# Gated decode attention: scores on TensorE from K with d on the partitions, and a softmax of partial maxima

## The chip, the cores and the metric

One Trainium2 chip, one of its cores. The metric is the device time of the whole kernel in microseconds, the median of several runs of one program. All arithmetic on the large tensors is float32.

## What is computed

One token goes through two attention blocks, and a gate mixes their outputs. Block A has 16 heads, each with its own K and V cache of 8192 keys; block B has 16 query heads that share 8 K and V caches, two heads to a cache. The head size is 256, the model width 448.

```python
x = A_x                                            # 1 x 1 x 448
g = sigmoid((x * gate_w).sum(-1, keepdims=True))
q = (x @ wq).reshape(16, 256)                      # in each block
p = softmax(q @ k.T * 256 ** -0.5)                 # over 8192 keys, each head
o = p @ v                                          # 256 numbers, each head
block = o.reshape(4096) @ wo
return g * A + (1 - g) * B
```

Each K and V cache of a head is 8 MB, and there are 24 of each, so 403 MB of caches and 29 MB of weights are read once and hardly any of it is used twice (only block B's, for two heads).

## The kernel before

The work is cut into 8 rounds `s`. A round has three units `u = (s, r)`: two heads of block A (`r` 0 and 1) and one cache of block B (`r` 2), with two query heads (`heads(u)` is 2 there). A unit's cache comes in four tiles `t` of 2048 keys, 2 MB each: 128 partitions with 16 keys (`ROWS`) of 256 numbers, 16 KB in one run on each partition. A round also needs a tile of `wq` (1792 KB; the first round's comes as two halves) and one of `wo` (1792 KB).

All these loads are issued by SyncE, in one list that lines 225 to 251 write out: K tiles run in `K_ORDER`, V tiles follow `LAG` = 7 tiles later in `V_ORDER`, and the next round's `wq` stands after the ninth K tile. Every tile gets the next of 11 slots of one ring (`slot`, line 72), so load n + 11 can be issued only when load n has been used. The loop at line 254 goes through the same list and writes down the work of the other engines in that order.

- `project` (line 130, TensorE): x, spread over 128 columns (`xb`, line 96), is the stationary operand and 256 columns of `wq` move, so that q appears alike on all partitions of PSUM.
- `score` (line 146, VectorE): for each of a tile's 16 keys per partition one `tensor_tensor_reduce` of 256 elements, K times q, summed into one column of `S`; two of them in block B. The profile shows each as two instructions, the operation and a read of its accumulator.
- `maximum` (line 157, VectorE), and `softmax` (line 163): GpSimd takes the maximum over the partitions (line 166) and makes it a bias, ScalarE computes Exp with a sum (line 172), GpSimd adds the sums over the partitions (line 174). One maximum stands for all 8192 keys of a head, so V can be used only when the unit's four K tiles have been scored.
- `weights` (line 178): the reciprocal of the sum times the gate, on partitions 0, 32, 64 and 96 (`pick`).
- `attend` (line 188, TensorE): for each of a tile's 16 keys per partition a column of `pr` is the stationary operand (1 or 2 columns) and 256 numbers of V move; the output goes to one of four partition groups (0, 32, 64, 96) of `o` in turn.
- `take` (line 199) copies `o` to SBUF, `finish` (line 203) adds the four groups with the weights and lays the result on the partitions, `emit` (line 213) multiplies by `wo` into `Y`, again in four groups of 112 columns.

At the end come the last V tile in three pieces of 8, 4 and 4 keys (`LAST_CUT`), two of four parts of the last `wo`, then `finish` and `emit` of the last unit, four copies of `Y` to one partition and the store (lines 309 to 319). A float32 matmul appears in the profile as two MATMUL and two LDWEIGHTS instructions.

## Time and profile before

| | |
|---|---|
| median of 3 runs | 1052.37 us (1052.14 to 1052.56) |
| the profiled execution, its own time | 1052.65 us |
| its span, first to last instruction | 1050.6 us |
| HBM read | 432.02 MB, 411 GB/s over the span |
| mean granted TensorE clock | 0.656 |
| engines' instructions | 13046 |

The page gives an engine's busy time, share of the span and count of instructions; for a DMA queue, its packets, megabytes and share of the time of 16 DMA engines. Queue q1 is SyncE's; the two queues called "instruction" bring the engines' own instructions. A stretch of time is one row: its bounds, its length, the busy time of PE (matmul), PEld (weight load), DVE (VectorE), ACT (ScalarE) and POOL (GpSimd) with their counts, the granted clock of TensorE, the mean share of the DMA engines that was busy, and GB/s. In a timeline a row is start, length, engine, line, operation, output and inputs, and in brackets the idle time before it and what ended it; equal instructions that follow each other are merged, with their count. SPq is the sequencer that issues SyncE's DMAs; for the DMA of a chain, the length is the time from issue to landing.

### The profile page before, as it was taken

How to read it: one execution, taken by the hardware profiler on the slowest of the kernel's cores; microseconds unless marked ns; L12 is line 12 of the kernel's file. 1: busy time of each engine (PE TensorE's matmuls, PEld its weight loads, DVE VectorE, ACT ScalarE, POOL GpSimd, SP SyncE). 2: the span in 40 equal slices, each digit the busy share in tenths (PEclk: the TensorE clock that was granted, in tenths of full speed). 3: DMA queues.
4: the chain of work that ended last, by engine and by line, in shares of the span. 5: the costliest groups of instructions: out<-in, count | busy, mean ns of one | idle time of the engine just before them, and what ended most of it. 6: DMA issues, size and time to landing. Idle time of an engine off the chain costs nothing.

```text
span 1050.6 us, 13046 instructions
## 1 busy us (share of the span) xinstructions
PE 430.7 (41%) x3969; PEld 184.2 (18%) x3969; DVE 721.3 (69%) x4187; ACT 26.1 (2%) x116; POOL 25.1 (2%) x77
## 2 busy tenths in 40 slices
PE   4053232733328333273433634336343353343355
PEld 3031010411105111041110411103111131011012
DVE  5998765686747867568675695855958559576760
ACT  0000000000000000000000000000000000000000
POOL 0000000000000000000000000000000000000000
PEclk8576566755556555576555876558666696666778
DMA  9999999999999999999999999999999999999971
GB/s 376 426 426 426 424 427 428 425 426 425 427 427 427 428 423 427 427 427 428 425 424 428 427 426 426 422 429 428 428 423 428 427 428 426 423 420 428 428 297 42
DMA packets 31031, 432.85 MB, mean 412 GB/s; under 512 B 3697, under 2 KB 3698, under 8 KB 4594
## 3 DMA queue, kind: packets, MB, share of 16 engines
q1 hardware_dynamic: 30818, 432.03, 97.5%
q8 instruction: 31, 0.51, 0.2%
q14 instruction: 38, 0.31, 0.1%
q10 hardware_dynamic: 144, 0.00, 0.0%
HBM read 432.02 MB, written 0.00 MB: 411 GB/s over the span
## 4 chain that ended last, share of the span: by engine, by line
DMA 88%; DVE 11%; PE 1%; issue 0%; ACT 0%; SPq 0%; ACTq 0%
DMA slot<-in_b_k_dram 42%; DMA slot<-in_a_v_dram 19%; DMA slot<-in_b_v_dram 15%; DMA slot<-in_a_k_dram 12%; DVE junk L153 10%; DMA slot<-in_wq_dram 0%; PE q L136 0%; DVE S L153 0%; PE o L196 0%; PE Y L218 0%; PE q L138 0%; PE sm L112 0%; PE sm L208 0%; DVE part L125 0%; DVE pick L126 0%
## 5 line engine op out<-in xcount | busy, mean ns | idle before, releaser
L153 DVE CUSTOM_DVE_ANT_0 junk<-slot,q 128x256 f32<-128x256 f32 x2048 | 705.6, 417 | 279.7 <-DMA slot<-in_a_k_dram 155.5
L196 PE MATMUL o<-slot,pr 128*1 128x256 f32 (+1 forms) x3072 | 318.6, 586 | 593.0 <-DMA slot<-in_a_v_dram 375.3
L196 PEld LDWEIGHTS o<-slot,pr 128*1 128x1 f32 (+1 forms) x3072 | 92.7, 111 | 785.8 <-issue 317.9
L153 DVE DVE_READ_ACCUMULATOR2_ANT S<- 128x1 f32 x2048 | 169.5, 83 | 0.0
L136 PE MATMUL q<-slot,xb 128*128 128x256 f32 x192 | 58.2, 448 | 23.5 <-DMA slot<-in_wq_dram 23.5
L136 PEld LDWEIGHTS q<-slot,xb 128*128 128x128 f32 x192 | 42.9, 228 | 36.4 <-DMA slot<-in_wq_dram 22.6
L201 ACT ACTIVATE osb<-o 128x256 f32<-128x256 f32 x24 | 9.2, 383 | 746.8 <-PE o L196 746.8
L138 PE MATMUL q<-slot,xb 128*128 128x256 f32 x64 | 21.3, 418 | 0.0
L208 PEld LDWEIGHTS sm<-sel,osb 128*128 128x128 f32 x96 | 17.7, 257 | 19.1 <-issue 17.1
L208 PE MATMUL sm<-sel,osb 128*128 128x1 f32 (+1 forms) x96 | 19.7, 309 | 0.6 <-ACT osb L201 0.6
L174 POOL PARTITION_ALL_REDUCE rs<-rs x24 | 9.7, 404 | 407.3 <-ACT pr L172 313.0
L218 PE MATMUL Y<-slot,ocs 128*1 128x112 f32 x512 | 17.6, 300 | 0.3 <-ACT ocs L210 0.3
L166 POOL PARTITION_ALL_REDUCE mx<-mx x24 | 9.0, 373 | 355.9 <-DVE mx L160 346.5
L182 DVE RECIPROCAL rc<-rs 128x1 f32<-128x1 f32 (+1 forms) x24 | 3.8, 159 | 19.2 <-POOL rs L174 19.2
L138 PEld LDWEIGHTS q<-slot,xb 128*128 128x128 f32 x64 | 13.9, 217 | 2.4
L218 PEld LDWEIGHTS Y<-slot,ocs 128*1 128x1 f32 x512 | 13.6, 95 | 2.2 <-issue 0.5
L168 POOL TENSOR_SCALAR nm<-mx 128x1 f32<-128x1 f32 (+1 forms) x24 | 6.2, 257 | 235.8 <-issue 235.8
L172 ACT ACTIVATE pr<-S,nm 128x64 f32<-128x64 f32 x32 | 10.9, 342 | 37.0 <-POOL nm L168 37.0
L318 DVE COPY ys<-Y 1x112 f32<-1x112 f32 x2 | 0.5, 266 | 14.2 <-PE Y L218 14.2
L210 ACT ACTIVATE ocs<-sm 128x2 f32<-128x2 f32 (+1 forms) x24 | 4.1, 172 | 225.8 <-PE sm L208 225.8
L103 PE MATMUL o<-zero 128*128 128x256 bf16 x24 | 8.1, 338 | 0.0
L115 DVE TENSOR_SCALAR ge<-ge 128x1 f32<-128x1 f32 x1 | 0.2, 154 | 9.6 <-ACT ge L114 9.6
(25 smaller groups left out, 27.3 us busy)
## 6 DMA issues: line engine op xcount, KB each, us to landing
slot<-in_a_k_dram SPq DMA_DIRECT2D x64, 2048.0 KB, 40.1
slot<-in_a_v_dram SPq DMA_DIRECT2D x64, 2048.0 KB, 40.0
slot<-in_b_k_dram SPq DMA_DIRECT2D x32, 2048.0 KB, 39.6
slot<-in_b_v_dram SPq DMA_DIRECT2D x31, 2048.0 KB, 40.1
slot<-in_wq_dram SPq DMA_DIRECT2D x7, 1792.0 KB, 38.9
slot<-in_wo_dram SPq DMA_DIRECT2D x7, 1792.0 KB, 39.5
slot<-in_wq_dram SPq DMA_DIRECT2D x2, 896.0 KB, 10.6
slot<-in_b_v_dram SPq DMA_DIRECT2D x1, 1024.0 KB, 34.0
```

Of the source, the lines that this page charges most:

```text
L103: nc.tensor.matmul(t[:, :n], zero[:, :P], zero[:, :n], start=True, stop=False, skip_group_check=True)
L136: nc.tensor.matmul(qe, xb[:, c], w[:, c * n + e * DH:c * n + (e + 1) * DH], start=(c == 0), stop=False)
L138: nc.tensor.matmul(qe, xb[:, KF + e], w[:, KF * n:KF * n + DH], start=False, stop=True)
L153: nc.vector.tensor_tensor_reduce(jk, kt[:, j, :], Q[u][:, m * DH:(m + 1) * DH], 1.0, 0.0, OP.mult, OP.add, S[u][:, m, c0 + j:c0 + j + 1])
L166: nc.gpsimd.partition_all_reduce(mx[:, 1, :M], mx[:, 0, :M], P, bass.bass_isa.ReduceOp.max)
L168: nc.gpsimd.tensor_scalar(nm[:, :M], mx[:, 1, :M], -scale, None, op0=OP.mult)
L172: nc.scalar.activation(pr[:, :, m], S[u][:, m, :], AF.Exp, bias=nm[:, m:m + 1], scale=scale, accum_out=rs[:, 0, m:m + 1])
L174: nc.gpsimd.partition_all_reduce(rs[:, 1, :M], rs[:, 0, :M], P, bass.bass_isa.ReduceOp.add)
L196: nc.tensor.matmul(O[u][32 * g:32 * g + M, :], PR[u][:, col, :M], vt[:, j, :], start=False, stop=(col >= NCOL - NG), skip_group_check=True)
L201: nc.scalar.activation(OB[u], O[u], AF.Copy)
L208: nc.tensor.matmul(oc[:, e, :M], o[:, e::2], SEL[u][:, :M], start=True, stop=True)
L218: nc.tensor.matmul(Y[32 * g:32 * g + 1, :], OC[u][:, e, m:m + 1], wt[:, h, e, g * YN:(g + 1) * YN], start=False, stop=(last and m == heads ...
```

## The change

- **K's layout.** The host lays K out anew (`turned`): a tile is still 2048 keys and 16 KB in one run on each of 128 partitions, but a partition now holds one of 128 positions of d, for both halves `e` of d and for four groups `g` of 512 keys. V stays as it was.
- **q.** `project` has the weights as the stationary operand (128 x 128) and a column of x as the moving one, so that q comes with d on the partitions. VectorE multiplies it by -1/16 and puts it into the middle of a tile of zeros (`QB`).
- **Scores.** For each tile 8 matmuls: 32 columns of `QB` are stationary and 512 keys of K move; the four groups go to four partition groups of one PSUM tile. The columns are cut out so that the head's q falls on row `t * M + m` of the group: each tile of the unit and each head has a row of its own.
- **Softmax.** Each row gets its own maximum (here a minimum, since the scores have the other sign): VectorE reduces the 512 columns, and ScalarE computes Exp with that bias and the row's sum. GpSimd's two reductions go. `turn` transposes the exponentials by four matmuls with a selecting matrix (`SELT`), which leaves zeros in the rows of other tiles; VectorE copies the result to `pr`.
- **Attend.** The stationary operand has 4 columns (8 in block B), one for each tile and head, so that every tile and group adds into a row of its own of `o`.
- **Putting together.** After a unit's last tile, `gather`, `combine` and `column` bring the 16 minima and sums of a head together, weigh them and lay the weights on the partitions, one step later each; `reduce_o` is what `finish` was, with VectorE's copy in place of ScalarE's.
- **Order.** K and V tiles alternate: K tile i, then V tile i - 1, with the units in the order 2, 0, 1. TensorE's order in step i is scores of tile i, attend of tile i - 1, turn of tile i, then projections and what is due. The last unit is one of block A, and one part of the last `wo` follows the last V piece instead of two.
- **Small.** x is loaded from ScalarE's queue; at the end one copy takes all of `Y`, and the store reads four partitions.

```diff
-LAG = 7
-K_ORDER = [(0, 0), (0, 1), (0, 2), (0, 3), (2, 0), (1, 0), (1, 1), (2, 1), (1, 2), (1, 3), (2, 2), (2, 3)]
-V_ORDER = [(0, 0), (0, 1), (0, 2), (0, 3), (1, 0), (1, 1), (1, 2), (1, 3), (2, 0), (2, 1), (2, 2), (2, 3)]
+UNITS = [2, 0, 1]
...
+    for M in (2, 1):
+        R = M * NT
+        SELT[M] = const.tile([P, NT, NG, R], F32, name=f"selt{M}")
+        nc.vector.memset(SELT[M], 0.0)
+        for t in range(NT):
+            nc.vector.tensor_copy(SELT[M][:, t, :, t * M:(t + 1) * M], one_of[:, :, t * M:(t + 1) * M])
+        MASK[M] = const.tile([P, NT], F32, name=f"mask{M}")
+        nc.vector.tensor_reduce(MASK[M], row_of[:, :R].rearrange("p (t m) -> p t m", m=M), axis=AX.X, op=OP.add)
...
+        for m in range(M):
+            h = m if r == 2 else r
+            for e in range(2):
+                for c in range(KF):
+                    at = c * n + h * DH + e * P
+                    nc.tensor.matmul(q[:, e, m:m + 1], w[:, at:at + P], xs[:, c:c + 1], start=(c == 0), stop=False)
+                at = KF * n + e * P
+                nc.tensor.matmul(q[:, e, m:m + 1], w[:, at:at + P], xs[:, KF + h:KF + h + 1], start=False, stop=True)
+        qb = QB[s % 2, r]
+        nc.vector.tensor_scalar(qb[:, :, 16:16 + M], q[:, :, :M], -scale, None, op0=OP.mult)
...
+        sc = ps_sc.tile([P, NC4 * P], F32, name="sc")
+        qb = QB[u[0] % 2, u[1]]
         for e in range(2):
...
+            for g in range(NG):
+                nc.tensor.matmul(sc[32 * g:32 * (g + 1), :], qb[:, e, 16 - t * M:48 - t * M], kt[:, e, g, :],
+                                 start=(e == 0), stop=(e == 1), skip_group_check=True)
+        st = ST[u]
+        nc.vector.tensor_reduce(st[:, 0, t:t + 1], sc, axis=AX.X, op=OP.min)
+        px = small.tile([P, NC4 * P], F32, name="px")
+        nc.scalar.activation(px, sc, AF.Exp, bias=st[:, 0, t:t + 1], scale=-1.0, accum_out=st[:, 1, t:t + 1])
+        PX[u, t] = px
...
+        for c in range(NC4):
+            nc.tensor.matmul(pt[:, c, :, :R], px[:, c * P:(c + 1) * P], SELT[M][:, t], start=True, stop=True)
+        pr = small.tile([P, NC4, NG, 2 * NT], F32, name="pr")
+        nc.vector.tensor_copy(pr[:, :, :, :R], pt[:, :, :, :R])
+        PR[u, t] = pr
...
+        pr = PR[u, t]
+        for j in range(j0, j0 + n):
+            c, g = divmod(j, NG)
+            nc.tensor.matmul(O[u][32 * g:32 * g + R, :], pr[:, c, g, :R], vt[:, j - j0, :],
+                             start=False, stop=(t == NT - 1 and c == NC4 - 1), skip_group_check=True)
...
+    def gather(u):
+        M = heads(u)
+        gs = small.tile([P, 2, NT], F32, name="gt")
+        nc.vector.tensor_tensor(gs, ST[u], MASK[M][:, None, :].to_broadcast([P, 2, NT]), op=OP.mult)
+        GS[u] = small.tile([P, 2], F32, name="gs")
+        nc.vector.tensor_reduce(GS[u], gs, axis=AX.X, op=OP.add)
+
+    def combine(u):
+
+        M = heads(u)
+        gi = 1 if u[1] == 2 else 0
+        T = ps_s.tile([1, 2, P], F32, name="sm")
+        for k in range(2):
+            nc.tensor.matmul(T[:, k, :], GS[u][:, k:k + 1], ident, start=True, stop=True)
...
+        for m in range(M):
+            nc.vector.tensor_reduce(mn[:, m:m + 1], of_head(T[:, 0, :], m), axis=AX.XY, op=OP.min)
+        for m in range(M):
+            nc.scalar.activation(ew[:, m], of_head(T[:, 0, :], m), AF.Exp, bias=mn[:, m:m + 1], scale=-1.0)
+        for m in range(M):
+            nc.vector.tensor_tensor(es[:, m], ew[:, m], of_head(T[:, 1, :], m), op=OP.mult)
+        nc.vector.tensor_reduce(z[:, :M], es[:, :M], axis=AX.XY, op=OP.add)
+        rz = small.tile([1, 2], F32, name="rz")
+        nc.vector.reciprocal(rz[:, :M], z[:, :M])
+        nc.vector.tensor_scalar(rz[:, :M], rz[:, :M], gate[:, gi:gi + 1], None, op0=OP.mult)
+        for m in range(M):
+            nc.vector.tensor_scalar(of_head(WR[M][:, m, :], m), ew[:, m], rz[:, m:m + 1], None, op0=OP.mult)
...
+        for m in range(M):
+            nc.tensor.matmul(cl[:, m:m + 1], WR[M][:, m, :], one, start=True, stop=True)
+        SEL[u] = small.tile([P, 2], F32, name="sel")
+        nc.vector.tensor_copy(SEL[u][:, :M], cl[:, :M])
...
+    for i in range(N + 1):
+
+        if i == 0:
+            load_wq(0, 1)
+        if i < N:
+            load_k(i)
+        if i == 2:
+            load_wq(0, 0)
+        if i % PER == 5 and i // PER + 1 < NS:
+            load_wq2(i // PER + 1)
+        if 0 < i < N:
+            load_v(i - 1)
+        if i % PER == 2 and i > PER:
+            load_wo(i // PER - 1, [(0, 4)])
+        if i == N:
+            load_wo(NS - 1, [(2, 4), (0, 1)])
+            VT[N - 1] = []
+            j0 = 0
             for n in LAST_CUT:
...
+                vt = slot([n, DH], "v")
+                nc.sync.dma_start(vt, v_src(N - 1)[:, j0:j0 + n, :])
+                VT[N - 1].append((j0, n, vt))
+                j0 += n
+            load_wo(NS - 1, [(1, 2)])
...
+        if i == 0:
+            project((0, 2), W[0, 1])
+            prepare()
+        if i < N:
+            scores(*work[i], KT.pop(i))
+        if i == N:
+            u = work[N - 1][0]
+            combine(u)
+            column(u)
+            emit((u[0], 2), WO[u[0]])
+            emit((u[0], 0), WO[u[0]])
+        if i > 0:
+            u, t = work[i - 1]
+            for j0, n, vt in VT.pop(i - 1):
+                attend(u, t, j0, n, vt)
+            PR.pop((u, t))
+            if t == NT - 1:
+                take(u)
+        if i < N:
+            u, t = work[i]
+            turn(u, t)
+            if t == NT - 1:
+                gather(u)
+                if i < N - 1:
+                    at(i + 1, combine, u)
+                    at(i + 2, column, u)
+                    at(i + 3, reduce_o, u)
...
+        s = i // PER + 1
+        if s < NS:
+            for k, r in enumerate(UNITS):
+                if i % PER == 6 + k:
+                    project((s, r), W[s, 1 if r == 2 else 0])
...
+        for f, args in later.pop(i, []):
+            f(*args)
+        if i % PER == 4 and i > PER:
+            for k, r in enumerate(UNITS):
+                emit((i // PER - 1, r), WO[i // PER - 1])
...
+    reduce_o((s, 1))
+    emit((s, 1), WO[s], last=True)
+
+    ys = const.tile([P, YN], F32, name="ys")
+    nc.vector.tensor_copy(ys, Y)
+    nc.sync.dma_start(out.rearrange("a b (g n) -> (a b g) n", g=NG), ys[::32, :])
```

More of the change, by code (lines that the diff above doesn't have):

```diff
@@ L94 @@
     nc.vector.memset(xs[KR:, KF:KF + 1], 0.0)
-    xb = const.tile([P, KF + 2, P], F32, name="xb")
-    nc.vector.tensor_copy(xb, xs[:, :, None].to_broadcast([P, KF + 2, P]))
-    junk = [const.tile([P, DH], F32, name=f"junk{i}") for i in range(3)]
-    gate = const.tile([P, 2], F32, name="gate")
-    pick = const.tile([P, 2], F32, name="pick")
+    gate = const.tile([1, 2], F32, name="gate")
     def clear(t, n):
@@ L117, in prepare @@
         nc.vector.tensor_scalar(gate[:, 1:2], gate[:, 0:1], -1.0, 1.0, op0=OP.mult, op1=OP.add)
-        nc.vector.memset(pick, 0.0)
-        row = const.tile([P, 2], F32, name="row")
-        nc.gpsimd.iota(row, pattern=[[-1, 2]], base=0, channel_multiplier=1,
-                       allow_small_or_imprecise_dtypes=True)
-        part = const.tile([P, 2], F32, name="part")
-        for c in range(NG):
-            nc.vector.tensor_scalar(part, row, float(32 * c), None, op0=OP.is_equal)
-            nc.vector.tensor_add(pick, pick, part)
@@ L178, in weights, with project @@
-    def weights(u):
+    KT, VT, SC, ST, PX, PR, O, GS, SEL, OB, OC = ({} for _ in range(11))
+    def project(u, w):
+        s, r = u
+        M = heads(u)
+        q = ps_s.tile([P, 2, 2], F32, name="sm")
+        n = 2 * DH
+        for m in range(M):
[8 more added lines that the diff above has]
+        nc.vector.tensor_scalar(qb[:, :, 16:16 + M], q[:, :, :M], -scale, None, op0=OP.mult)
@@ new lines, in turn, with attend @@
+    def turn(u, t):
+        M = heads(u)
+        R = M * NT
+        pt = ps_t.tile([P, NC4, NG, 2 * NT], F32, name="pt")
+        px = PX.pop((u, t))
+        for c in range(NC4):
[3 more added lines that the diff above has]
+        PR[u, t] = pr
+    def attend(u, t, j0, n, vt):
+        R = heads(u) * NT
+        if t == 0 and j0 == 0:
+            O[u] = ps_o.tile([P, DH], F32, name="o")
+            clear(O[u], DH)
+        pr = PR[u, t]
[3 more added lines that the diff above has]
+                             start=False, stop=(t == NT - 1 and c == NC4 - 1), skip_group_check=True)
@@ L179, in weights, with take @@
+    def take(u):
+        OB[u] = small.tile([P, DH], F32, name="osb", bufs=3)
+        nc.scalar.activation(OB[u], O[u], AF.Copy)
+    def gather(u):
+        M = heads(u)
+        gs = small.tile([P, 2, NT], F32, name="gt")
[3 more added lines that the diff above has]
+    def combine(u):
         M = heads(u)
         gi = 1 if u[1] == 2 else 0
-        rc = small.tile([P, 2], F32, name="rc")
@@ L204, in finish, with reduce_o @@
+    def reduce_o(u):
         M = heads(u)
@@ L309 @@
-    finish((NS - 1, 2))
-    emit((NS - 1, 2), W[NS - 1], last=True)
-    ys = const.tile([1, D], F32, name="ys")
-    for g in range(NG):
-        part_y = ys[:, g * YN:(g + 1) * YN]
-        if g % 2:
-            nc.scalar.activation(part_y, Y[32 * g:32 * g + 1, :], AF.Copy)
-        else:
-            nc.vector.tensor_copy(part_y, Y[32 * g:32 * g + 1, :])
-    nc.sync.dma_start(out.rearrange("a b n -> (a b) n"), ys)
+    work = [((s, r), t) for s in range(NS) for r in UNITS for t in range(NT)]
@@ new lines, with load_wq, load_wq2, load_k @@
+    N = len(work)
+    PER = len(UNITS) * NT
+    W, WO = {}, {}
+    def load_wq(s, pair):
+        w = slot([WQ], "wq")
+        nc.sync.dma_start(w, wq[s][:, pair * WQ:(pair + 1) * WQ])
+        W[s, pair] = w
+    def load_wq2(s):
+        w = slot([2 * WQ], "wq")
+        nc.sync.dma_start(w, wq[s])
+        for pair in range(2):
+            W[s, pair] = w[:, pair * WQ:(pair + 1) * WQ]
+    def load_k(i):
+        u, t = work[i]
+        kt = slot([2, NG, NC4 * P], "k")
+        nc.sync.dma_start(kt, of(u, a_k, b_k)[t])
+        KT[i] = kt
@@ new lines, in v_src, with load_v, load_wo, at @@
+    def v_src(i):
+        u, t = work[i]
+        return of(u, a_v, b_v)[t * ROWS * P:(t + 1) * ROWS * P, :].rearrange("(p j) d -> p j d", p=P)
+    def load_v(i):
+        vt = slot([ROWS, DH], "v")
+        nc.sync.dma_start(vt, v_src(i))
+        VT[i] = [(0, ROWS, vt)]
+    def load_wo(s, parts):
+        if s not in WO:
+            WO[s] = slot([4, 2, D], "wo")
+        for h0, h1 in parts:
+            nc.sync.dma_start(WO[s][:, h0:h1], wo[s][:, h0:h1])
+    later = {}
+    def at(step, f, *args):
+        later.setdefault(step, []).append((f, args))
@@ L322 @@
+    assert not later
+    s = NS - 1
+    reduce_o((s, 1))
[3 more added lines that the diff above has]
+    nc.sync.dma_start(out.rearrange("a b (g n) -> (a b g) n", g=NG), ys[::32, :])
 _OUTS = [((1, 1, D), "float32")]
```

207 lines of the change are left out of this document (54 added, 153 removed).

## The prediction

> **What bounds the kernel now.** I read the page first (engines, DMA queues, the chain that ended last), then the stretches, then SyncE's issues against the packets of the instruction queues, and last the final 40 us piece by piece.
>
> ```profile
> PE 430.7 (41%) x3969; PEld 184.2 (18%) x3969; DVE 721.3 (69%) x4187; ACT 26.1 (2%) x116; POOL 25.1 (2%) x77
> ...
> q1 hardware_dynamic: 30818, 432.03, 97.5%
> q8 instruction: 31, 0.51, 0.2%
> q14 instruction: 38, 0.31, 0.1%
> ...
> DMA 88%; DVE 11%; PE 1%; issue 0%; ACT 0%; SPq 0%; ACTq 0%
> ```
> ```profile
> 1010.00:1015.00 5.00, 3.25 (x45) 1.27 (x36) 4.03 (x25) 0.17 (x1) 0.38 (x1) 0.94 0.87 310
> ...
> 200.00:1000.00 800.00, 333.26 (x3035) 138.96 (x3035) 553.00 (x3208) 17.97 (x84) 19.25 (x56) 0.64 1.01 426
> ```
>
> The columns of a stretch are the busy time of PE, PEld, DVE, ACT and POOL, then the TensorE clock, the DMA share and GB/s. From 200 to 1000 us all 16 DMA engines are busy (share 1.01) at 426 GB/s: 26.7 GB/s each. The chain is 88% DMA. So making VectorE (69% busy) lighter is worth nothing by itself, unless it changes when the stream of 432.03 MB ends.
>
> Now the end of the stream: first the last 1 MB piece of V in the chain, then SyncE's last issues, then stretches.
>
> ```profile
> 1007.19 33.97 DMA slot<-in_b_v_dram
> ```
> ```profile
> 1021.84 5.25 SPq L284 DMA_DIRECT2D slot<-in_wo_dram  x2
> 1048.61 0.32 SPq L319 DMA_DIRECT2D out_dram<-ys  x1
> ```
> ```profile
> 1022.00:1022.80 0.80, 0.80 (x20) 0.38 (x16) 0.00 (x0) 0.00 (x0) 0.00 (x0) 1.00 0.15 61
> ...
> 1025.20:1026.60 1.40, 0.00 (x0) 0.00 (x0) 0.00 (x0) 0.00 (x0) 0.00 (x0) 1.00 0.08 35
> 1031.00:1041.00 10.00, 5.17 (x64) 1.72 (x64) 0.39 (x2) 0.00 (x0) 0.41 (x1) 0.83 0.06 26
> ```
>
> From 1031 to 1041 us the chip moves 26 GB/s, a share of 0.06: **one** engine of 16 is still working, alone. It lands the 1 MB piece at 1007.19 + 33.97 = 1041.16 and then has its share of two 512 KB and two 448 KB pieces left, 1.966 MB / 16 / 26 GB/s = 4.7 us: its stream ends at 1045.9. The others wait for nothing but issues: at 1022.0 to 1022.8 two or three are busy (0.15 x 16 = 2.4), at 1025.2 to 1026.6 only one (0.08 x 16 = 1.3). So by 1025.2 the second-latest engine had all that was issued, that is all but the last 448 KB (1.07 us): it would have ended by 1026.3, and not before 1022.8 + 2.1 = 1024.9, since until 1022.8 more than one still worked on V, with both 448 KB pieces to come. I take 1025.2. One engine is 20.7 us behind the next.
>
> Why it is behind: each issue of SyncE waits for an earlier landing, and a load has landed when its last engine has, so the spacing of the issues is the pace of the slowest engine.
>
> ```profile
> SPq L290 <- DMA slot<-in_a_v_dram: 192.0, 42, 5.5
> ```
> ```profile
> 400.76 0.33 SPq L272 DMA_DIRECT2D slot<-in_b_k_dram  x1
> 406.62 0.33 SPq L290 DMA_DIRECT2D slot<-in_a_v_dram  x1
> 411.50 0.33 SPq L272 DMA_DIRECT2D slot<-in_a_k_dram  x1
> 416.40 0.33 SPq L290 DMA_DIRECT2D slot<-in_a_v_dram  x1
> 421.29 0.33 SPq L266 DMA_DIRECT2D slot<-in_wq_dram  x1
> 426.19 0.33 SPq L272 DMA_DIRECT2D slot<-in_a_k_dram  x1
> ```
>
> Steps of 4.88 to 4.90 us, but one of 5.86: 0.96 us more. Queues asked by stretch, 400.5 to 402 us and then 405 to 408, show what fell there:
>
> ```profile
> q14 instruction: 1, 0.01, 1.3%
> ```
> ```profile
> q8 instruction: 1, 0.02, 2.2%
> ```
>
> The long step holds the one q14 packet; the q8 packet leaves its step at 4.88. By size q8 carries TensorE's instructions (0.51 MB over 2 x 3969 is 64 bytes each). At 64 bytes a q14 packet (0.31 MB / 38 = 8 KB) is 128 instructions, and VectorE's 4187 need 33 of the 38. 33 x 0.96 = 31.7 us: the fetches of VectorE's instructions, all by one DMA engine, account for its lag. Were all engines even, 432.03 MB at 426 GB/s from about 1.6 us on would end near 1016, 30 us before 1045.9.
>
> **The change part by part.** *VectorE's instruction stream.* Removed: 2048 tensor_tensor_reduce, each with a read of the accumulator (4096 of the 4187). Added: 96 minima, 96 copies of pt, 24 x 2 gather, 16 x 6 + 8 x 9 combine, 24 + 24 column and reduce_o copies, 24 project, some 32 at the start: about 512, or 4 blocks. That engine's lag falls to 4 x 0.96 = 3.8 us, so it would end at 1045.9 - 27.9 = 1018, and the engine at 1025.2 is late next. Term: **-20.7 us**; ends 0 (it is slow for another reason) and -30 (the others' lag goes too).
>
> *TensorE's instruction stream.* Matmuls: scores 768, attend 1536, turn 384, project 256, emit 256, combine, column and reduce_o 128, others 4, all f32 and two each: 6,664 with 25 bf16 clears near 6,700 against 3969. Fetches go from 31 to 52. In the trace 31 made no engine later than 1026.3, 10 us after the even end: at most 0.33 us each on one engine, 21 more at most 7. The q8 packet above did not touch the slowest, and about three engines were late together, so I think them spread: **+1.0**, ends 0 and +7.
>
> *TensorE's own work*, per step (a K tile and a V tile; 24 loads of 4.89 and two of 7/8 size in 12 steps make 10.5 us):
>
> ```profile
> 1007.27 3.51 PE L196 MATMUL o<-slot,pr 128*1 128x256 f32 x32 [6.92 <-DMA slot<-in_a_v_dram]
> ...
> 1012.06 1.91 PE L196 MATMUL o<-slot,pr 128*1 128x256 f32 x32 [0.72 <-DMA slot<-in_a_v_dram]
> ...
> 1044.31 1.25 PE L196 MATMUL o<-slot,pr 128*2 128x256 f32 x16
> 1046.12 0.63 PE L208 MATMUL sm<-sel,osb 128*128 128x2 f32 x4 [0.56 <-ACT osb L201]
> 1047.02 0.95 PE L218 MATMUL Y<-slot,ocs 128*1 128x112 f32 x32 [0.26 <-ACT ocs L210]
> ```
> ```profile
> 12.02 1.01 PE L112 MATMUL sm<-gw,xb 128*128 128x1 f32 x8
> ```
>
> Attend keeps its 32 instructions: 1.91 to 3.51. Scores: 16 of 512 columns into four partition groups, the same columns, so the same if four overlap as attend's do (0.06 us each). Turn: 8 with a 128x128 weight, the L112 row: 1.0. Project: 512 in all at 0.126: 0.7 a step. reduce_o, emit, combine, column: 0.5. Sum 6.0 at the fast end; times 3.51 / 1.91, 11.0 at the slow end. Cover at 6.0: the stream's 10.5. Without it each step costs the excess (rivals). Lowering TensorE's slack adds nothing in the middle: **0**.
>
> *New waits.* turn waits on TensorE for scores, minimum and Exp; behind it queue project and the next scores. The minimum takes 512/640 of the row below, 0.66 us, an Exp of 512 I estimate alike: 1.4 us, beside attend of the tile before (1.91). If that cover is gone, 1.4 of 4.5 us slack. combine, column and reduce_o each come a step later, when their operands are done. GpSimd's reductions go from a queue that was not on the path: 0.
>
> ```profile
> 2.87 0.82 DVE L96 COPY xb<-xs 128x640 f32<-128x640 f32 x1
> ```
>
> *The ring.* The wq tile of a round is load n; its last projection comes after attend of load n+7, and load n+11 reuses its slot. At that landing three loads are queued, 14.7 us of the slowest engine's work. TensorE needs attend, turn and 16 of project, 4.9 us (9.6 at the slow end) and an issue some 2 us (1048.61 to the end of the span): cover 3.1 us at worst. If TensorE is 6 us late besides, 7 x 2.9 = 20 us. **+0.5**, ends 0 and +20.
>
> *Head.* x moves to ScalarE's queue, so the first weight load starts 0.46 us sooner: **-0.5**, ends -0.5 and 0.
>
> ```profile
> 0.72 0.40 SPq L85 DMA_DIRECT2D xs<-in_x_dram  x1
> 1.18 0.41 SPq L259 DMA_DIRECT2D slot<-in_wq_dram  x1
> ```
>
> *Tail.* Behind the last V piece comes one wo part instead of two (it lands 1.07 us later in the stream); attend is no longer behind 32 of emit (it began at 1044.31, 0.6 after the landing that 1045.9 - 2.1 gives), the last emit has 16 instead of 32 (0.5 less), one copy goes instead of two in a row. -0.2. Against it, combine, column and 48 of emit stand ahead of the last attend, 3 to 4 us of TensorE in 5.6 us between V landings: up to +1.5. **0**.
>
> Sum on the profiled execution: 1050.6 - 20.7 + 1.0 + 0.5 - 0.5 = 1030.9 us of span; 1052.65 is 2.05 above its span, and 0.28 above the median of 1052.37: 1030.9 + 2.05 - 0.28 = **1032.7 us**.
>
> **Rivals.** *Slower: TensorE's clock makes it the bound.* Its place is every step, the price 11.0 us of TensorE against 10.5 of stream, so 96 x 11.0 + 13 to the first scores (the L112 row, ahead of them, ends at 13.0) + 7 from the last V landing to the end = 1076 us. It decides once the mean clock falls under about 0.55.
>
> ```profile
> 10.00:13.00 3.00, 3.00 (x18) 2.56 (x16) 0.00 (x0) 0.00 (x0) 0.00 (x0) 1.00 1.00 426
> 18.70:21.50 2.80, 2.77 (x7) 2.24 (x8) 2.80 (x19) 0.00 (x0) 0.00 (x0) 0.50 1.04 445
> ```
>
> For it: 0.64 over the middle, and 0.50 at 18.7 while busy. Against it: 1.00 at 10 and 0.94 at 1010, after work without pause; a TensorE that falls behind has no pauses left and speeds up. The Trainium skill, page "TensorE: Matmul & The Clock Gate", section "Why this matters for your kernels", says that idle gaps over some 3 us put the clock back to half; waits between K and V landings here are of that length, so by that rule alone this rival would win at 1076. Chance 0.05. *Scores that do not overlap* would put TensorE over 10.5 too (each above 0.40 us against 0.12): 0.02, beyond 1100.
>
> *No change*: the engine is slow by its place, the fetch steps a coincidence. Then 1052.4 + 1.0 + 0.5 - 0.5 = 1053.4. For it: only one long step is shown here. Against it: the count, 31.7 us by fetches against 30 of lag. Page "DMA: Bandwidth & Descriptors", section "Latency and other measured facts", of the Trainium skill has engines 7 and 15 as usually slower; by that the lag would stay. The rows (even 4.89, and 5.86 with the packet) speak for the fetch. Chance 0.05.
>
> *Part of it is given back*: TensorE's fetches fall on a late engine (+6 more), or the ring holds (+1 to 3 for each of 7): about 1041. Nothing shows which engines serve q8. Chance 0.11.
>
> *More*: the next engines' lag was VectorE's doing too; then even engines, 1025.2 - 1016 = 9 us less: 1023. Chance 0.05.
>
> **How the numbers follow.** Forecast 0.72, at 1032.7; its own terms reach from 1030 to 1037. The range takes in the partly given back case and half the way to the larger gain: 1027 to 1041. Within 0.2% (2.1 us, about what a measurement of this kernel can tell from no change): 0.04, most of the no-change case. Faster by more: 0.72 + 0.11 + 0.05 = 0.88. Slower: 0.05 + 0.02 + the rest of no change 0.01 = 0.08.
>
> **What would show it.** q14 falls from 38 packets to under 12, q8 rises to about 52; SyncE's steps stay at 4.89 us with few of 5.86; the stretch in which one engine works alone falls from 20 us to under 5; VectorE under 15% busy; TensorE over 60% and its clock over 0.7; the middle still at 426 GB/s. Wrong if the lonely stretch stays with q14 gone (place), if the middle falls under 420 GB/s (ring or TensorE), or if SyncE's steps lengthen with q8 packets.

## The result, and the profile after

The changed kernel takes **1033.95 us** (median of 4 runs, 1031.03 to 1034.28); the kernel before, run beside it on the same chip, 1052.26 us (1050.85 to 1052.56). The ratio is 0.9822 (95% interval 0.9803 to 0.9842), so it is faster by 18.3 us. The profiled execution is the quickest of the four: 1031.03 us, with a span of 1029.3 us. Line numbers below are those of the changed kernel, and in the views of an experiment those of its own kernel.

The page of the changed kernel answers the first rows of the prediction: engines, queues, chain, and the costliest groups of instructions (busy us and mean ns of one, then idle time before and what ended it).

```profile
PE 781.1 (76%) x6689; PEld 386.3 (38%) x6689; DVE 139.2 (14%) x512; ACT 93.0 (9%) x250; POOL 0.6 (0%) x6
...
q1 hardware_dynamic: 30680, 432.03, 98.9%
q8 instruction: 52, 0.85, 0.3%
q14 instruction: 11, 0.08, 0.0%
...
DMA 92%; PE 8%; issue 0%; DVE 0%; ACT 0%; ACTq 0%; SPq 0%
...
L199 PE MATMUL o<-slot,pr 128*4 128x256 f32 (+1 forms) x3072 | 258.8, 495 | 162.5 <-DMA slot<-in_a_v_dram 99.9
L172 PE MATMUL sc<-slot,qb 128*32 128x512 f32 x1536 | 276.1, 847 | 72.3 <-DMA slot<-in_b_k_dram 43.6
```

VectorE has exactly the 512 instructions of the prediction, q14 has 11 packets instead of 38, q8 has 52 instead of 31. The kernel is still bound by its 432.03 MB: 92% of the chain is DMA, and TensorE's 781.1 us are 8.1 us in each of 96 steps, under the stream's 10.5.

The issues of SyncE in the same view as before (start, length, engine, line, operation):

```profile
33.68 0.33 SPq L288 DMA_DIRECT2D slot<-in_a_k_dram  x1
38.57 0.33 SPq L297 DMA_DIRECT2D slot<-in_a_v_dram  x1
43.47 0.33 SPq L288 DMA_DIRECT2D slot<-in_a_k_dram  x1
```

Every step shown is 4.89 or 4.90 us, and so are most of the others. From 30 to 980 us nine steps take 5.5 to 6.8 us, where the kernel before has 28 of 5.8 us or more, all of them with a q14 packet. But of the nine, seven hold a q8 packet, as in this one (the packet is from the queues between 336 and 342.1 us):

```profile
335.92 0.33 SPq L288 DMA_DIRECT2D slot<-in_a_k_dram  x1
342.14 0.33 SPq L297 DMA_DIRECT2D slot<-in_a_v_dram  x1
```
```profile
q8 instruction: 1, 0.02, 1.0%
```

That step is 6.22 us, 1.3 more than the others. The prediction named steps that lengthen with q8 packets as a sign that it would be wrong, and for about one q8 packet in seven the sign is there.

The stretches from 1008 to 1024 us (bounds, length, PE, PEld, DVE, ACT, POOL with counts, clock, DMA share, GB/s):

```profile
1008.00:1012.00 4.00, 4.00 (x22) 2.59 (x26) 0.39 (x2) 0.00 (x0) 0.00 (x0) 0.50 0.97 400
1012.00:1016.00 4.00, 3.82 (x45) 1.30 (x37) 0.69 (x1) 0.78 (x2) 0.00 (x0) 0.85 0.61 248
1016.00:1020.00 4.00, 1.71 (x24) 1.28 (x27) 1.67 (x10) 0.27 (x1) 0.00 (x0) 1.00 0.50 199
1020.00:1024.00 4.00, 4.00 (x74) 2.55 (x68) 0.00 (x0) 0.00 (x0) 0.00 (x0) 0.57 0.21 83
```

The stretch in which one engine worked alone (a share of 0.06, from about 1031 us to 1045.9 in the kernel before) is gone. In its place stands a step of 0.50 from 1016 to 1020 us: **eight** of the 16 DMA engines are still at work, at 199 / 8 = 25 GB/s each, while the other eight have finished. What they still move after 1020 is 83 GB/s x 4 us = 332 KB, 1.6 us at 199 GB/s, so they end together, within some 3 us. The trace says the same load by load: it keeps 16 landing events for each load, taken here as one for each DMA engine. For the last load of all, a part of `wo`, eight come from 1011.9 to 1016.0 us and the other eight from 1021.2 to 1022.9. The stream ends 23.0 us earlier than the 1045.9 of before, where the prediction had 19.7 (20.7 - 1.0 - 0.5 + 0.5).

The end of the chain of waits of the changed kernel, from the last V tile but one:

```profile
974.36 39.17 DMA slot<-in_a_v_dram
1013.66 1.91 PE o L199 x32
1015.57 1.01 PE pt L186 x8
...
1017.15 0.61 PE sm L219 x4
...
1019.45 0.35 PE sm L245 x2
1019.80 2.14 PE Y L264 x48
1021.94 2.57 PE o L199 x32
...
1024.53 0.39 ACT osb L204
```

It does not run through the last landing. It leaves the stream at 974.36 + 39.17 = 1013.53 us and stays with the other engines: attend, turn, the sums of `gather` and `combine`, `column`, 48 matmuls of `emit`, and only then the last attend, which ends at 1024.5. The last V piece lands at 1021.8 by its landing events (the `wo` part of 1022.9 comes behind it). The eight matmuls that need this piece take some 0.6 us, so behind the landing alone they would end at about 1022.5: some 2 us of this execution belong to the tail. A second profile of the same kernel (e0 below, a run of 1033.99 us) shows how a run of that length comes about:

```profile
974.39 39.12 DMA slot<-in_a_v_dram
1013.64 3.56 PE o L199 x32
...
1021.65 2.35 PE Y L264 x48
1024.00 2.11 PE o L199 x17
```

The landing is the same to 0.02 us (1013.51), but the attend that follows takes 3.56 us instead of 1.91, and the span is 1032.2 instead of 1029.3. The granted clock of that stretch is what differs, first in the quicker execution, then in the second:

```profile
1013.60:1017.00 3.40, 2.90 (x40) 1.77 (x40) 1.02 (x4) 0.78 (x2) 0.00 (x0) 1.00 0.56 228
```
```profile
1013.60:1017.20 3.60, 3.56 (x33) 1.09 (x33) 0.00 (x0) 0.00 (x0) 0.00 (x0) 0.53 0.55 224
```

1.00 against 0.53. TensorE had idled 3.05 us for that landing in the second execution and 0.18 in the first; whether that is why the clock differs is not shown. From the landing at 1013.5 to the end of the span the tail takes 15.8 us in one execution and 18.7 in the other.

### The profile page after: what moved, and what is told of

Read it like the earlier page. It is cut to its first block, busy times and chain, and to the rows that moved or that the text cites. A ratio compares the mean times of both kernels' runs of the same rounds, so it can differ in the third digit from the quotient of the medians.

```text
span 1029.3 us, 14842 instructions
## 1 busy us (share of the span) xinstructions
PE 781.1 (76%) x6689; PEld 386.3 (38%) x6689; DVE 139.2 (14%) x512; ACT 93.0 (9%) x250; POOL 0.6 (0%) x6
## 3 DMA queue, kind: packets, MB, share of 16 engines
q1 hardware_dynamic: 30680, 432.03, 98.9%
## 4 chain that ended last, share of the span: by engine, by line
DMA 92%; PE 8%; issue 0%; DVE 0%; ACT 0%; ACTq 0%; SPq 0%
DMA slot<-in_a_v_dram 50%; DMA slot<-in_b_k_dram 23%; DMA slot<-in_b_v_dram 15%; DMA slot<-in_a_k_dram 4%; PE o L199 3%; PE sm L158 1%; PE sc L172 1%; PE pt L186 1%; DMA gw<-in_gate_w_dram 1%; PE sm L160 1%; PE sm L254 0%; PE Y L264 0%; PE sm L245 0%; PE sm L219 0%; ACTq L84 0%
## 5 line engine op out<-in xcount | busy, mean ns | idle before, releaser
L199 PE MATMUL o<-slot,pr 128*4 128x256 f32 (+1 forms) x3072 | 258.8, 495 | 162.5 <-DMA slot<-in_a_v_dram 99.9
L172 PE MATMUL sc<-slot,qb 128*32 128x512 f32 x1536 | 276.1, 847 | 72.3 <-DMA slot<-in_b_k_dram 43.6
L199 PEld LDWEIGHTS o<-slot,pr 128*4 128x4 f32 (+1 forms) x3072 | 92.3, 104 | 368.2 <-issue 272.7
L177 ACT ACTIVATE px<-sc,st 128x512 f32<-128x512 f32 x96 | 66.0, 687 | 802.0 <-DVE st L175 802.0
L186 PEld LDWEIGHTS pt<-selt,px 128*128 128x128 f32 x768 | 115.0, 230 | 62.2 <-issue 52.1
L186 PE MATMUL pt<-selt,px 128*128 128x16 f32 (+1 forms) x768 | 125.2, 302 | 1.6 <-ACT px L177 1.6
L172 PEld LDWEIGHTS sc<-slot,qb 128*32 128x32 f32 x1536 | 56.3, 134 | 166.6 <-issue 85.2
L175 DVE TENSOR_REDUCE st<-sc 128x1 f32<-128x512 f32 x96 | 66.4, 692 | 299.5 <-PE sc L172 299.5
L158 PE MATMUL sm<-xs,slot 128*128 128x1 f32 x384 | 62.7, 279 | 5.7 <-DMA xs<-in_x_dram 5.7
L158 PEld LDWEIGHTS sm<-xs,slot 128*128 128x128 f32 x384 | 59.5, 231 | 5.7 <-DMA xs<-in_x_dram 5.7
L160 PE MATMUL sm<-xs,slot 128*128 128x1 f32 x128 | 28.1, 289 | 0.0
L160 PEld LDWEIGHTS sm<-xs,slot 128*128 128x128 f32 x128 | 25.2, 244 | 0.0
```

Source lines behind the costliest of these rows:

```text
L158: nc.tensor.matmul(q[:, e, m:m + 1], w[:, at:at + P], xs[:, c:c + 1], start=(c == 0), stop=False)
L160: nc.tensor.matmul(q[:, e, m:m + 1], w[:, at:at + P], xs[:, KF + h:KF + h + 1], start=False, stop=True)
L172: nc.tensor.matmul(sc[32 * g:32 * (g + 1), :], qb[:, e, 16 - t * M:48 - t * M], kt[:, e, g, :], start=(e == 0), stop=(e == 1), skip_group_ ...
L175: nc.vector.tensor_reduce(st[:, 0, t:t + 1], sc, axis=AX.X, op=OP.min)
L177: nc.scalar.activation(px, sc, AF.Exp, bias=st[:, 0, t:t + 1], scale=-1.0, accum_out=st[:, 1, t:t + 1])
L186: nc.tensor.matmul(pt[:, c, :, :R], px[:, c * P:(c + 1) * P], SELT[M][:, t], start=True, stop=True)
```

## The experiments

"The theory" is the prediction's: a DMA engine that also brings an engine's instructions falls behind in the loads by a fixed time per block of instructions (one packet of an instruction queue), and the latest of the 16 engines sets the end. The rivals are that VectorE's work itself was the limit, that the slow engine was slow by its place, and that a changed order of loads or a lighter GpSimd made the gain. Medians are over 4 runs each, 5 for e8. The runs were taken in three groups (e0 to e3; e4, e5, e6 and e10; e7, e8, e9 and e11), and the kernel before took 1052.43, 1053.25 and 1052.63 us beside them, so a difference under a microsecond between groups says nothing. The added writes, reductions and one-element matmuls of e1 to e6 and e11 go to a scratch tile or add zeros: nothing of the computation is left out or changed by them.

### e0_after: the changed kernel again

> The changed kernel once more, as the base for the runs beside it. Expected by both theories: 1031 to 1035 us; q8 52 packets, q14 about 11.

1033.23 us (1031.14 to 1034.04), ratio 0.9816 (0.9801 to 0.983): as expected, and the base for the rest.

### e1_dve_4128, e2_dve_2016, e3_dve_768: VectorE's instructions back, without the work

```diff
+    tick = const.tile([1, 1], F32, name="tick")
...
             turn(u, t)
+            for _ in range(43):
+                nc.vector.memset(tick, 0.0)
```

(21 and 8 in place of 43 for e2 and e3.)

> The changed kernel with 43 writes of one number by VectorE in each of the 96 steps: 4128 more instructions that read nothing and take some 60 ns each (250 us of an engine that is 86% idle). Fetch theory (each block of 128 VectorE instructions costs 0.96 us of one DMA engine): 32 more blocks, 31 us more on that engine; it stood some 6 to 7 us ahead of the latest ones at the end, so the stream ends 24 us later: 1058 us (1052 to 1062), one DMA engine alone for the last 20 us, q14 about 43 packets. Rival theory (what counted was VectorE's large reads of K beside the transfers): no change, 1031 to 1035 us.

> The same with 21 writes in each step, 2016 more instructions, 16 blocks. Fetch theory: 15 us more on that engine, of which 6 to 7 are hidden behind the engines that are latest now: 8 us later, 1042 us (1038 to 1045), q14 about 27 packets. Rival theory: no change, 1031 to 1035 us.

> The same with 8 writes in each step, 768 more instructions, 6 blocks. Fetch theory: 5.8 us more on that engine, hidden behind the latest ones: no change, within 1 us of the changed kernel beside it. A theory in which every VectorE instruction delays the whole stream in proportion (31 us for 4128) expects 5.8 us more, 1037 to 1041 us. The theory of large reads expects no change.

| | q14 packets | median us | ratio (95%) |
|---|---|---|---|
| e0 | 10 | 1033.23 | 0.9816 (0.9801 to 0.983) |
| e3 | 16 | 1036.28 (1033.48 to 1037.67) | 0.9844 (0.9827 to 0.9862) |
| e2 | 26 | 1045.65 (1045.03 to 1047.3) | 0.9939 (0.9924 to 0.9954) |
| e1 | 42 | 1063.87 (1062.35 to 1064.08) | 1.0106 (1.0089 to 1.0122) |

With 43 one-element writes a step the kernel is slower than the one before, though VectorE is busy for only a third of the time. Its page and its last stretches show why:

```profile
PE 758.3 (71%) x6689; PEld 376.1 (35%) x6689; DVE 365.7 (34%) x4640; ACT 92.6 (9%) x250; POOL 0.6 (0%) x6
...
q14 instruction: 42, 0.34, 0.1%
```
```profile
1032.00:1036.00 4.00, 3.21 (x28) 1.84 (x27) 1.59 (x26) 0.00 (x0) 0.00 (x0) 0.95 0.06 25
1036.00:1040.00 4.00, 0.92 (x12) 0.29 (x12) 1.81 (x21) 0.78 (x2) 0.00 (x0) 0.90 0.06 25
...
1044.00:1048.00 4.00, 0.00 (x0) 0.00 (x0) 2.08 (x36) 0.00 (x0) 0.00 (x0) 0.75 0.06 25
```

The lonely engine is back: a share of 0.06 and 25 GB/s for over 12 us, made by instructions alone. The three doses fit one line. Some six of the q14 packets come before or beside the loads (by the landing events the changed kernel's 10 or 11 leave that engine about 4 us behind); at 0.96 us for each of the rest the lag is 0.96 x (26 - 6) = 19 us in e2 and 35 us in e1. The landing events give the same price: the late engine's last landing is at 1033.1 us in e2 and at 1048.65 in e1, 0.97 us for each of 16 packets. What counts is only what exceeds the eight late engines, about 11 us behind: +8 for e2, +24 for e1, and nothing for e3 (9.6 us). Measured are +12.4, +30.6 and +3.1. All three medians lie above their expected bounds (1062, 1045 and 1 us over e0). About 2 us is a slower stream in all of these kernels (see e11), and the rest stands at the end, where the writes of the last step are queued ahead of `gather` (in e1 42 of them take 4.73 us there, 0.11 each, so 0.9, 2.4 and 4.8 us). With both the sums are +2.9 for e3, +12.4 for e2 and +30.8 for e1. These two terms were found after the runs.

### e4_dve_busy: VectorE's work back, without the instructions

```diff
...
+            nc.vector.tensor_reduce(tick, ident[:, None, :].to_broadcast([P, 32, P]), axis=AX.XY, op=OP.add)
```

One reduction of 4.41 us in each of the 96 steps.

> The changed kernel with one long VectorE reduction of 4096 elements per partition in each step: 96 instructions more, but some 4.3 us each, 410 us of VectorE in all. Fetch theory: not one block more than 96/128 = 0.75, so the stream ends as in the changed kernel, 1032 to 1037 us (the reduction also stands in front of the last step's short operations, up to 4 us at the very end). Rival theory (VectorE's busy time or reads beside the transfers): VectorE back over 50% busy, half of the gain and more is lost, over 1042 us.

1039.46 us (1038.53 to 1041.04), ratio 0.9876 (0.9861 to 0.9891). Between the two expectations. VectorE is busier than in e1 and the kernel 24 us faster:

```profile
PE 752.0 (73%) x6689; PEld 371.5 (36%) x6689; DVE 541.2 (52%) x608; ACT 92.7 (9%) x250; POOL 0.6 (0%) x6
```
```profile
1018.55 4.41 DVE L359 TENSOR_REDUCE tick<-ident 128x1 f32<-128x4096 f32 x1
1022.88 0.15 DVE L209 TENSOR_TENSOR gt<-st,mask 128x8 f32<-128x8 f32 x1
```

The second fence is VectorE's timeline at the end: the last reduction stands in front of `gather` and holds the tail of the chain for 4.4 us. With that and the 2 us of the stream, the +6.2 are accounted for. No cost of VectorE's busy time in the steps is left to see.

### e10_before_few: the kernel before with fewer, longer VectorE instructions

In three of the four tiles of block A the 16 scores are made four at a time, by a multiplication into a [P, 4, DH] tile and a reduction, in place of `tensor_tensor_reduce`:

```diff
...
+        if u[1] < 2 and c0 < 3 * ROWS:
+            for j in range(0, n, 4):
+                nc.vector.tensor_tensor(prod, kt[:, j:j + 4, :], Q[u][:, None, :].to_broadcast([P, 4, DH]), op=OP.mult)
+                nc.vector.tensor_reduce(S[u][:, 0, c0 + j:c0 + j + 4], prod, axis=AX.X, op=OP.add)
+            return
```

> The kernel before, with the scores of three of four tiles of block A by one multiplication and one sum for four keys at a time, in place of one fused operation and a read for each key: 1152 VectorE instructions fewer (9 blocks), but some 24 x 48 / 12 = 100 us more VectorE work. Fetch theory: 9 x 0.96 = 8.6 us sooner, 1044 us (1042 to 1046), although VectorE is busier. Rival theory (VectorE's work and reads): same or slower than before, over 1052 us.

1043.77 us (1042.84 to 1044.47), ratio 0.9914 (0.9898 to 0.9931): 9.5 us faster than the kernel before, which took 1053.25 beside it. The page:

```profile
PE 436.1 (42%) x3969; PEld 186.7 (18%) x3969; DVE 921.2 (88%) x3035; ACT 26.6 (3%) x116; POOL 25.1 (2%) x77
...
q8 instruction: 31, 0.51, 0.2%
q14 instruction: 29, 0.24, 0.1%
```

VectorE went **up** from 721.3 to 921.2 us, the layout, the order of the loads, GpSimd's part and TensorE's stream are as before, and nine q14 packets fewer at 0.96 are 8.6 us. This rules out VectorE's load, the order and an engine that is slow by its place as the cause of these 9.5 us.

### e5_pe_6144: more instructions for TensorE

```diff
+            for _ in range(32):
+                nc.tensor.matmul(Y[:1, :1], zero[:, :1], zero[:, :1], start=False, stop=False, skip_group_check=True)
```

> The changed kernel with 32 matmuls of one element (bf16, two instructions each) in each step, 6144 more TensorE instructions, 24 blocks of 256: q8 76 packets for 52. Theory that TensorE's blocks take turns on eight DMA engines, 1.4 us each: 3 more on each, 4.2 us later, 1037 to 1039 us. If one late engine got them all: 24 x 1.4 = 34 us, 1067 us. If TensorE's fetches cost nothing: no change but what TensorE itself loses, 1033 to 1035 us.

1038.08 us (1034.35 to 1038.76), ratio 0.9854 (0.9834 to 0.9874); expected were 1037 to 1039 for eight engines that take turns, and 1067 for one engine. q8 has 76 packets, 24 more than the changed kernel. In the chain of waits the same V tile lands 4.7 us later, at 1018.19 instead of 1013.53:

```profile
977.57 40.62 DMA slot<-in_a_v_dram
1018.33 3.42 PE o L199 x32
```
```profile
1016.00:1020.00 4.00, 1.67 (x18) 0.61 (x21) 0.58 (x1) 0.78 (x2) 0.00 (x0) 0.50 0.49 203
1020.00:1024.00 4.00, 4.00 (x64) 2.47 (x56) 0.46 (x3) 0.00 (x0) 0.00 (x0) 0.82 0.50 204
```

The plateau with half of the DMA engines at work is longer: it holds through 1020 to 1024, where the changed kernel has already fallen to 0.21. Of the last load's landing events eight come from 1011.9 to 1015.9, as in the changed kernel, and the other eight from 1025.9 to 1027.6, each 4.7 us later than there. The 24 blocks on eight engines are three each; 4.7 / 3 = 1.6 us per block, 16 KB each by size. By that, the changed kernel's 52 blocks (6.5 on each of the eight) are 10 us, about the 11 from the first landing events of its last load at 1011.9 to the last at 1022.9.

### e6_pool_4128: the writes on GpSimd

The 43 writes of e1, with `nc.gpsimd.memset`.

> The changed kernel with the 43 writes in each step on GpSimd in place of VectorE. Fetch theory, if a block of another engine's instructions costs the same and all of an engine's blocks use one DMA engine: 32 more q14 packets, a lag of 31 us on one DMA engine, some 20 to 25 us later, 1053 to 1060 us. If only VectorE's stream costs: 1031 to 1035 us.

1046.2 us (1044.92 to 1046.62), ratio 0.9936 (0.9922 to 0.9951): slower than e0 by 13.0 us, as the theory has it and VectorE's part cannot explain, but under the expected 1053 to 1060.

```profile
1028.00:1032.00 4.00, 3.01 (x32) 1.51 (x20) 0.62 (x4) 0.17 (x1) 0.00 (x0) 0.88 0.06 26
1032.00:1036.00 4.00, 2.70 (x54) 2.23 (x57) 1.04 (x6) 0.10 (x1) 0.00 (x0) 0.55 0.05 19
```
```profile
100.00:400.00 300.00, 217.56 (x1905) 107.01 (x1897) 38.49 (x138) 25.85 (x70) 182.06 (x2045) 0.77 1.01 426
...
700.00:1000.00 300.00, 211.90 (x2031) 104.99 (x2031) 40.28 (x143) 27.94 (x76) 0.00 (x0) 0.82 1.01 426
```

One engine works alone here too; its last landing is at 1035.5 us, 10.6 behind the eight. GpSimd, which waits for nothing, ran ahead and did all its writes before 700 us (the column before the clock). Why its blocks cost less than VectorE's was not settled.

### e8_tail, e7_pair, e9_pair_tail: what can be had back

e8 puts the last `column` behind the two `emit`, so that 48 matmuls fill the time in which TensorE waits for the sums; e7 lets one attend matmul take two keys of a partition (512 numbers move, the output has two halves that `reduce_o` adds), which takes TensorE's instructions from 6689 to 5321 matmuls; e9 does both.

```diff
             combine(u)
-            column(u)
             emit((u[0], 2), WO[u[0]])
             emit((u[0], 0), WO[u[0]])
+            column(u)
```

> The changed kernel with one line moved: in the last step the 48 emit instructions stand between combine and column, where TensorE waits 1.7 us for VectorE's short operations, and no longer between column and the last attend. If the end of the changed kernel is set by TensorE's queue behind the last landing: the last attend begins about 2 us sooner, 1031 us (1030 to 1033). If the end is set by the last landing: no change, 1033 to 1034 us.

> The changed kernel with attend in pairs: two keys of a group in one matmul (twice the columns of weights, 512 numbers of V moving), each result half used, so the same streaming time and 2736 TensorE instructions fewer: q8 41 packets for 52. Theory that eight DMA engines share TensorE's blocks at 1.4 us each: 1.4 fewer on each, 1.9 us sooner in the stream, 0.6 us lost at the end to a longer copy and two more matmuls: 1032 us (1031 to 1034). If TensorE's blocks cost nothing: 1033.5 to 1035 us.

> Both together, the version that the runs so far point to. If stream and tail add: 1030 us (1028.5 to 1031.5).

| | q8 | median us | ratio (95%) | span of the profile |
|---|---|---|---|---|
| e0 | 52 | 1033.23 (1031.14 to 1034.04) | 0.9816 (0.9801 to 0.983) | 1032.2 |
| e7 | 42 | 1032.92 (1032.0 to 1034.15) | 0.9816 (0.9802 to 0.9829) | 1030.1 |
| e8 | 52 | 1029.92 (1029.22 to 1032.85) | 0.9793 (0.9778 to 0.9807) | 1028.0 |
| e9 | 42 | 1028.86 (1028.27 to 1031.45) | 0.9781 (0.9767 to 0.9795) | 1026.6 |

e7 alone cannot be told from e0: with ten blocks fewer its loads end at 1021.4 us instead of 1022.9, but the end is held by the tail. e8's median is 3.3 us lower with the same stream (2.4 us by the ratios, whose intervals overlap by a hair), and its last attend starts at 1021.40 in the chain, where e0's starts at 1024.00. e9's median is 4.4 us lower; and with both, the chain goes through the landing of the last V piece:

```profile
996.20 24.31 DMA slot<-in_a_v_dram
...
1020.55 0.66 PE o L204 x8
...
1021.23 0.61 ACT osb L209
```

So the last V piece of e9 lands at 1020.51, and of the changed kernels only here is the stream the last thing that the last attend waits for.

### e11_dve_768_even: a surprise

e3's 8 writes a step, placed ahead of `turn` instead of behind it, and a scratch tile of 64 bytes on its partition in place of 4:

```diff
+    tick = const.tile([1, 16], F32, name="tick")
...
+            for _ in range(8):
+                nc.vector.memset(tick[:, :1], 0.0)
             turn(u, t)
```

> The changed kernel with 768 more VectorE instructions as before (8 in each step), but the scratch tile has 64 bytes instead of 4 on its partition, so that the ring behind it starts at a multiple of 64 bytes as in the changed kernel, and they stand ahead of turn, not ahead of gather. Fetch theory (5.8 us hidden behind the latest engines) and a stream slowed in the earlier runs by the ring's uneven start: 1033 to 1034.5 us, 427 GB/s in the middle. If the 768 instructions slow the whole stream by themselves: 1035 to 1037 us and 426 GB/s as in the earlier run.

**1023.66 us** (1023.62 to 1024.85), ratio 0.973 (0.9716 to 0.9743): the fastest kernel of all, and outside all that was expected. It was to settle e3's 2 us, and it points to a cause that no theory here had in this size. The gain is in the whole stream, not at the end. First SyncE's issue of the first piece of the last V tile, in the changed kernel, e3 and e11, then one stretch of the middle of each in the same order:

```profile
989.04 10.12 SPq L331 DMA_DIRECT2D slot<-in_a_v_dram  x3
```
```profile
990.89 10.15 SPq L332 DMA_DIRECT2D slot<-in_a_v_dram  x3
```
```profile
981.89 10.01 SPq L332 DMA_DIRECT2D slot<-in_a_v_dram  x3
```
```profile
700.00:1000.00 300.00, 231.47 (x1971) 114.77 (x1967) 40.15 (x141) 27.45 (x74) 0.00 (x0) 0.74 1.01 427
```
```profile
700.00:1000.00 300.00, 216.94 (x1945) 105.58 (x1945) 49.61 (x362) 26.66 (x72) 0.00 (x0) 0.78 1.01 426
```
```profile
700.00:1000.00 300.00, 227.28 (x1994) 109.74 (x1986) 52.13 (x373) 27.44 (x74) 0.00 (x0) 0.76 1.01 430
```

427, 426 and 430 GB/s, with the DMA engines fully busy in all three, and the issue 1.85 us later in e3 and 7.15 us earlier in e11. The bytes are the same. What differs between these programs for the loads is where the ring's 11 slots start on their partitions, since the scratch tile lies ahead of them. In the built programs:

| kernels | first slot starts at byte | past a multiple of 256 | GB/s from 100 to 1000 us |
|---|---|---|---|
| e11 | 23808 | 0 | 430 |
| changed kernel, e0, e8 | 23744 | 192 | 427 |
| e7, e9 | 25792 | 192 | 427 |
| e5 (24 more blocks of instructions) | 23744 | 192 | 426 |
| e1, e2, e3, e4, e6 | 23776 | 224 | 426 (e1 425 in one stretch) |
| kernel before | 24672 | 96 | 426 |
| e10 | 28768 | 96 | 426 |

The slots are 16 KB apart, so all 11 share the remainder. Over these 14 runs the rate goes with it, but for e5. The engines that land first, and so are not held back by instructions, show it more sharply, by the first landing event of the last load: 1011.9 us in the changed kernel, e0, e8 and in e5 too, though e5 has 6144 more instructions; 1012.1 in e7 and e9; 1013.7 and 1013.8 in e3 and e4, whose additions differ and whose rings both start 32 bytes further on; 1005.1 in e11. So added instructions alone do not move these engines. That the ring's place does is still an argument and not shown: no run moves the ring and nothing else, and e11 also has its writes in another place. The Trainium skill, page "DMA: Bandwidth & Descriptors", section "How a descriptor splits into AXI transactions", says that a descriptor that doesn't start at a multiple of 256 bytes needs one transaction more and spends time on the bytes before its start. It speaks of bytes that are fetched, while the ring is where these loads write, so it need not be the mechanism here. The direction agrees with the rows; the size does not follow its count of 32-byte beats: 192 and 224 past would be 6 and 7 beats on the 512 of 16 KB (1.2% and 1.4%) and measure 0.73% and 0.92% by the issues (989.04 and 990.89 against 981.89), and 96 past would be 3 beats (0.6%), but the kernel before is no faster than 224 past.

## Why the prediction was right, and where it was not

**What bounds the kernel, and the main term: right in kind.** The forecast was 1032.7 us in a range of 1027 to 1041, and 1033.95 was measured. Instruction fetches hold back the DMA engine that makes them, and the latest engine sets the end. e1 and e2 bring the lag back with instructions that do nothing, e4 shows that VectorE's work without them does not, and e10 takes 9.5 us out of the kernel before while VectorE gets busier. 0.96 us a block of VectorE's stream served in all of them. One reading behind it was wrong: the q8 packet between 405 and 408 us began before 406.6, so it lies in the long step of 5.86 us too, beside the q14 packet, and not in the step of 4.88. The rest of that trace bears the conclusion out, since every one of its 28 steps of 5.8 us or more holds a q14 packet.

**"The engine at 1025.2 is late next": wrong for the changed kernel.** The latest engines of the changed kernel are the eight that share TensorE's blocks, and the loads end at 1022.9, where the prediction's sum had 1026.2. Of the 3.3 us, about 1.5 to 2 can be put down to the stream's rate, if the ring's place is its cause: the changed kernel's ring starts where 427 GB/s are seen and not 426, and e3, moved back to 426, issues 1.85 us later. The rest is that the engines that were late next in the kernel before are late no more. The landing events of the load that begins to land at about 813 us show this. In the kernel before four engines are together, eight are 2.8 to 5.1 us behind, three 10.3 to 11.2, and VectorE's 27.9. In the changed kernel eight are 7.7 to 9.5 us behind and none of the others more than 3.1. In e10, which has nine of VectorE's blocks fewer, the three are still 10.6 to 11.9 us behind, so VectorE's blocks are not what made them late. What did stays open: no view shows whose packets they were.

**"TensorE's fetches +1.0, at most 0.33 us each on one engine": the mis-sized term.** A block costs about 1.6 us of one engine (e5), and blocks go to eight engines in turn, so 21 more are 21 / 8 x 1.6 = 4.2 us. SyncE's steps of 6.2 us with a q8 packet, 1.3 us over the others, are the same price seen from the queue. The bound from the kernel before was drawn from the wrong engine: it took the time by which nobody was later than 10 us for the price of 31 blocks on one engine, where the eight engines at 2.8 to 5.1 us fit 22 blocks by 813 us, 22 / 8 x 1.6 = 4.4. The 4.2 us lie inside the term's ends of 0 and +7. The price was hidden in the forecast, since the engine it assumed to be next was not there: with the eight at the even end plus 10 us, the sum came out near. That is luck.

**"Tail 0, ends -0.2 and +1.5": the other miss.** The profiled execution ends 1029.3 - 1022.9 = 6.4 us after the last load, and the kernel before 1050.6 - 1045.9 = 4.7: +1.7. In executions with a lower clock at the end it is up to 3 us more (the second profile: 1032.2 with the same landing). The prediction counted 3 to 4 us of TensorE between the last two V landings; the chain shows 8.4 to 10.5 us from the landing at 1013.5 to the start of the last attend. `combine`, `column` and `emit` are 3.1 us of it (0.61, 0.35 and 2.14), as counted. What was left out is attend and turn of the tile before (2.9 us) and the small steps of VectorE and ScalarE around `combine` (from 1016.6 to 1019.45 above), for which `emit` had to wait too. e8 moved `emit` into that time and its median is 3.3 us lower.

**The sum.** For the profiled execution: -23.0 + 1.7 = -21.3 from 1050.6 is 1029.3, where 1030.9 was forecast. The median of 1033.95 lies 2.9 us over the profiled execution's 1031.03, where the forecast took the difference of before (0.28 under it), so 1032.7 came out 1.25 us low. The errors are -3.3 (the stream), +1.7 (the tail), -0.3 (time outside the span) and +3.2 (median against profiled execution); that they nearly cancel is luck, and the number is closer than its working.

**The small terms.** TensorE's work was 8.1 us a step against the forecast of 6.0 to 11.0: covered, as said. SyncE's waits for TensorE add up to some 8 us (the largest row: "SPq L288 <- PE sc L172", 4.2 us in 4 times), but the DMA share is 1.01 in the middle, so no loss by them is seen and +0.5 can't be told from nothing. The head's -0.5 can't be told apart from the stream's rate. The middle holds 427 GB/s.

**The rivals.** TensorE did not become the bound: its mean clock was 0.748, over the 0.55 that this rival needed. The Trainium skill, page "TensorE: Matmul & The Clock Gate", section "Why this matters for your kernels", puts the clock back to half after idle gaps of over some 3 us. This kernel hardly tests that, since TensorE's waits for K and V were mostly shorter (231.9 us in 110 waits, 2.1 each). Short waits did not keep the clock full either: from 1008 to 1012 us it was 0.50, with TensorE busy for all of the 4.00 us. Scores do overlap: 847 ns a matmul summed is 276.1 us busy over 1536, 0.18 us each. "No change" fell with e10. "Partly given back" had the right suspect, TensorE's blocks, with the wrong size. "More" had the lag of the next engines gone, as it went, but VectorE's blocks were not its cause (e10), and eight other engines stood in their place.

## What to carry to other kernels

When a kernel is a fully loaded stream, count the instructions of each engine and the packets of the instruction queues, and ask which DMA engines bring them: the time is that of the latest of the 16, and one-element instructions cost as much there as long ones. Read the last stretches by their DMA share times 16 (1 is one engine left, 8 is half of them) before anything is said about who is late, and follow the chain from the last landing but one, since a short list of small dependent steps can outlast the stream. Compare the GB/s of the middle to the last digit after any edit that moves tiles, since the stream of e11 gained 0.7% where nothing of the loads had been touched but their place (beside some added writes); e11 (1023.66 us) and e9 (1028.86 us) both beat the change, and the two together, with the ring at a multiple of 256 bytes and no added writes, were not tried.
